# A11 B11 of the transform's first two blocks in seven quarter products, with the gate and T1 of the last stage moved

## The chip, the cores and the metric

The kernel runs on one core of a Trainium2 chip. The metric is the device time of one execution in microseconds. The kernel before took 672.08 us as the median of 3 runs (671.87 to 673.23).

## What is computed

```python
a = einsum("bsd,ed->bse", x, dft_hid_re);  b = einsum("bsd,ed->bse", x, dft_hid_im)
y = einsum("ts,bse->bte", dft_seq_re, a) - einsum("ts,bse->bte", dft_seq_im, b)
up = einsum("bsd,df->bsf", x, w3);  gate = einsum("bsd,df->bsf", x, w1)
z = einsum("bsf,fd->bsd", silu(gate) * up, w2)
g = sigmoid((x * gate_w).sum(-1, keepdims=True))
out = g * y + (1 - g) * z
```

There are 2048 rows (S), 512 columns (D) and 1376 hidden columns of the SwiGLU half. Everything is float32, and w1, w3 and w2 are scaled up by 200.

## The kernel before, in words

Every product is computed in float32 accuracy from two parts of each operand, a high part (ScalarE, `high`, L110) and the rest (VectorE, `low`, L113). `mm3` (L126) then issues three matmuls for each product of tiles: high by high, high by low, low by high, in this order, with the streamed operand's low part first needed by the second of the three. One matmul is 128x128 by 128x512. Each large product is a 2x2 block product done with seven block products instead of eight: P1 to P7, of sums of blocks that are called T1, T2, T3 and T4.

**Stages.** The gate and up projection runs first, in 22 items (`gate_up`, L333), the last of which ends where the transform begins. Four blocks of 512 rows follow for the transform along S (`KIND` "F", blocks 0 to 3), then two blocks for the down projection ("H", 4 and 5), then two for the transform along D ("Y", 6 and 7). A block of the F stage has 28 steps: seven products of four steps each. A step is twelve matmuls on one streamed tile of 128x1024: four in the two halves of the tile by the two output banks, times three.

**The list of steps.** `STEPS` (L650) is written by a loop over blocks, and PE takes the steps in that order, which is also the program's order on every other engine (the schedule is manual). After step m the function `advance` (L755) loads the tile of step m+8 (SP), forms the sum of step m+4 (`sum_c`, VectorE, L723 and L727) and splits step m+3 (`split_c`, high on ScalarE and low on VectorE, into one of four `zo` tiles). So a `zo` tile of step m+3 is the one that step m-1 used. Work of other kinds is hung on steps with `at(blk, n, f)`: it is issued ahead of that step.

**Quarter products.** For blocks 2 and 3 the first product, P1 = A11 B11, isn't done block by block. A11 is the same for both, so the two products are one 2x2 product of quarters of A11 with the two B11, done in seven products m1 to m7 (`QUARTERS`, L645; each has two steps, a and b, of six matmuls) instead of the eight that two P1 hold. The table `AMONG` (L647) sets them between full steps of blocks 1 and 2. `step_quarter` (L913) issues them: m1 and m6, m7 and m4 accumulate in bank 5, and ScalarE copies that bank after m1 (to bank 4, on which m2 accumulates), after m6 and after m7 (to a tile `uu`). m5 goes to bank 7; VectorE then writes bank 6 = bank 7 - uu[0] and bank 7 = bank 7 - uu[1], and m3 accumulates on bank 6. `seeds` (L907) copies the two banks of a block for the later products. Two weights of these products are sums of columns of x (`load_s`, `sums_s`, `high_s`, `low_s`: two tiles `sr`, four subtractions or additions of 128x512 on VectorE, two splits). The streamed sums of quarters are made in DRAM by GpSimd's queue (`quarter_sum`, L440, with accumulating DMAs).

**The last item and the first steps.** In the last `gate_up` item VectorE adds u4 and bank X (L369), which PE must wait for before its last six matmuls on bank X (`prod(x, n, 6, 2, ...)`, L385), since these add to the same bank. Functions hung under `early` (L357) run ahead of that add.

**Results.** A block's four results are multiplied by the gate g on VectorE (`spill`, L947) and stored to DRAM (`zsp`); `load_gate` loads the gate. In the Y stage T1 = B12 + B11 is added on VectorE from two stored blocks.

## Time and profile before

| what | value |
|---|---|
| median of 3 runs | 672.08 us |
| the profiled execution | 671.68 us, of which its span is 669.8 us |
| PE busy | 665.3 us, 99%, 3089 matmuls |
| VectorE busy | 589.6 us, 88%, 699 instructions |
| ScalarE busy | 378.8 us, 57%, 483 instructions |
| DMA | 178.57 MB, 267 GB/s in the mean |
| mean granted TensorE clock | 1.000 |

All times of the trace count from the start of the span. In the timeline a row has its start, how long it lasted, the engine, the line of the kernel, the operation, what it wrote and read, and how often it follows itself; in brackets stands idle time before it and what ended that. Consecutive instructions of VectorE and ScalarE overlap by up to about 0.1 us in the records, so what one costs in a full queue is the distance between two starts. PE's records overlap likewise: six matmuls are shown as 1.46 us and start 1.29 us apart from the next six.

### The profile page before, as it was taken

What the parts mean: (1) busy time and instruction counts of PE and PEld (TensorE: products, weight loads), DVE (VectorE), ACT (ScalarE), POOL (GpSimd) and SP (SyncE); (2) the same over time, 40 slices, a digit from 0 to 9 for tenths busy, and PEclk for the clock granted to TensorE, in tenths of its full rate; (3) what the DMA queues carried; (4) which work ended last, traced back from release to release, by engine and by line L of the source; (5) the groups of instructions that cost most, each with busy time, mean ns of one, the idle gap of its engine ahead of it and who ended that gap; (6) DMA issues with size and microseconds to landing.
All of it is one profiled execution on the core that took longest, in us unless ns stands there. A gap on an engine that the chain in (4) does not pass through costs nothing.

```text
span 669.8 us, 8635 instructions
## 1 busy us (share of the span) xinstructions
PE 665.3 (99%) x3089; PEld 578.4 (86%) x3089; DVE 589.6 (88%) x699; ACT 378.8 (57%) x483; POOL 69.1 (10%) x122
## 2 busy tenths in 40 slices
PE   9999999999999999999999999999999999999997
PEld 6888888888888888888888888888888888888886
DVE  6979987787669999988999998999889799798896
ACT  6765556666546874475565664454447447445452
POOL 0112322221111000112000010001000010010000
PEclk9999999999999999999999999999999999999999
DMA  7789897999996956659668467619989857884942
GB/s 297 263 319 252 298 310 257 281 343 384 425 370 238 389 192 230 215 206 271 254 232 318 157 225 282 231 67 324 405 310 336 270 184 178 314 302 175 339 126 94
DMA packets 49338, 178.57 MB, mean 267 GB/s; under 512 B 5776, under 2 KB 7184, under 8 KB 45840
## 3 DMA queue, kind: packets, MB, share of 16 engines
q1 hardware_dynamic: 35296, 121.52, 51.0%
q0 software_dynamic: 13568, 55.85, 23.9%
q10 hardware_dynamic: 432, 0.66, 0.3%
q8 instruction: 24, 0.39, 0.2%
q14 instruction: 18, 0.15, 0.1%
HBM read 126.35 MB, written 60.04 MB: 278 GB/s over the span
## 4 chain that ended last, share of the span: by engine, by line
PE 99%; ACT 0%; issue 0%
PE P L124 56%; PE X L124 16%; PE quarter L124 12%; PE Z L124 8%; PE Y L124 4%; PE C L124 2%; PE wps L405 1%; PE V L124 0%; PE P4left L124 0%; ACT zc L974 0%
## 5 line engine op out<-in xcount | busy, mean ns | idle before, releaser
L110 ACT ACTIVATE zo<-B 128x1024 fp32r<-128x1024 f32 x178 | 181.0, 1021 | 171.8 <-DVE B L723 67.0
L113 DVE TENSOR_TENSOR zo<-B,zo 128x1024 fp32r<-128x1024 f32 x178 | 208.3, 1178 | 18.5 <-ACT zo L110 17.2
L124 PE MATMUL P<-zo,a 128*128 128x512 f32 x960 | 209.7, 379 | 0.0
L124 PEld LDWEIGHTS P<-zo,a 128*128 128x128 f32 x960 | 181.4, 189 | 25.9
L723 DVE TENSOR_TENSOR B<-B,B 128x1024 f32<-128x1024 f32 (+1 forms) x78 | 91.8, 1177 | 0.1
L124 PE MATMUL P<-zo,H 128*128 128x512 f32 x420 | 91.3, 379 | 0.0
L124 PEld LDWEIGHTS P<-zo,H 128*128 128x128 f32 x420 | 79.2, 189 | 11.8 <-issue 0.7
L124 PE MATMUL X<-xo,wb 128*128 128x512 f32 x378 | 88.7, 379 | 0.0
L124 PEld LDWEIGHTS X<-xo,wb 128*128 128x128 f32 x378 | 71.3, 189 | 10.4 <-DVE u L369 0.2
L124 PE MATMUL quarter<-zo,a 128*128 128x512 f32 x324 | 71.9, 379 | 0.0
L124 PE MATMUL P<-zo,Y 128*128 128x512 f32 (+1 forms) x336 | 71.6, 375 | 0.0
L124 PEld LDWEIGHTS P<-zo,Y 128*128 128x128 f32 x336 | 62.7, 189 | 8.7
L124 PEld LDWEIGHTS quarter<-zo,a 128*128 128x128 f32 x324 | 61.2, 189 | 8.7
L324 POOL DMA_DIRECT2D hsp<-h x40 | 22.3, 558 | 106.5 <-DVE h L375 61.5
L386 ACT ACTIVATE h<-X 128x512 f32<-128x512 f32 x21 | 12.5, 596 | 34.9 <-PE X L124 34.9
L124 PE MATMUL Z<-xo,wb 128*128 128x512 f32 x126 | 30.6, 379 | 0.0
L124 PE MATMUL Z<-xo,wa 128*128 128x512 f32 x126 | 30.6, 379 | 0.0
L727 DVE TENSOR_TENSOR B<-B,B 128x1024 f32<-128x1024 f32 (+1 forms) x26 | 30.6, 1178 | 0.0
L124 PE MATMUL X<-xo,wa 128*128 128x512 f32 x126 | 30.5, 379 | 0.0
L124 PE MATMUL Y<-xo,wa 128*128 128x512 f32 x126 | 30.5, 379 | 0.0
L124 PEld LDWEIGHTS Y<-xo,wa 128*128 128x128 f32 x126 | 23.8, 189 | 3.4
L124 PEld LDWEIGHTS Z<-xo,wb 128*128 128x128 f32 x126 | 23.8, 189 | 3.4
(181 smaller groups left out, 662.1 us busy)
## 6 DMA issues: line engine op xcount, KB each, us to landing
B<-cc SPq DMA_DIRECT2D x64, 512.0 KB, 5.6
hsp<-h POOLq DMA_DIRECT2D x40, 256.0 KB, 6.7
wbsp<-wb POOLq DMA_DIRECT2D x8, 1024.0 KB, 5.8
wb<-wbsp SPq DMA_DIRECT2D x8, 1024.0 KB, 8.2
B<-hsp SPq DMA_DIRECT2D x16, 512.0 KB, 8.1
B<-zsp SPq DMA_DIRECT2D x16, 512.0 KB, 8.7
tsp<-cc POOLq DMA_DIRECT2D x12, 512.0 KB, 9.0
ws<-w SPq DMA_DIRECT2D x11, 512.0 KB, 6.4
```

The costliest lines, as they stand in the source:

```text
L110: nc.scalar.activation(hi, src, AF.Copy)
L113: nc.vector.tensor_sub(lo, src, hi.bitcast(F32))
L124: nc.tensor.matmul(ps.rearrange("p (n a) -> p n a", a=2), u, turns(v)[:, some], **kw)
L324: nc.gpsimd.dma_start(hsp[g, b + k, j // 2, :, j % 2 * 512 : (j % 2 + 1) * 512], h)
L386: nc.scalar.activation(g1, x, AF.Silu)
L405: nc.tensor.matmul(wps, warm[:, :P], warm, start=True, stop=True)
L723: nc.vector.tensor_add(t, t, RAW[blk, b, q][:, :n])
L727: nc.vector.tensor_sub(t, RAW[blk, "B12", q][:, :n], t)
```

## The change

The first products of blocks 0 and 1 are now done as those of 2 and 3 are: `AMONG` gets three entries for block 0, and the loop leaves P1 out for all F blocks.

- Block 0's own P1 had been the first four steps of the stage. Now m1a, m1b, m2a and m2b come first, then two steps of P5 (T1), then m6a, m6b, m7a, m7b, the third step of P5, then m4a, m4b, m5a, m5b, m3a, m3b, and the fourth.
- Each group follows without a full step in between, unlike those of blocks 2 and 3, which keep their places.
- The sums of x for the weights are loaded at the end of item 19 (`load_s0`), and VectorE makes them (`sums_s`) under `early` of the last item. They are split by `high_s` and `low_s` at steps of block 0.
- `quarter_sum` makes 32 sums instead of 16, with other places on GpSimd's queue: 16 during the gate and up projection, 16 at steps of blocks 0 and 1.
- The gate of blocks 0 and 1 is no longer multiplied in there (`PLAIN`); it is done in block 6. The stored B12 of the Y stage is already T1: an accumulating DMA adds it into `zt1` in DRAM, so VectorE's T1 sums of blocks 6 and 7 are gone.
- One late part of w2 moves from block 1 to the end of block 3, where it goes straight into its tile.
- `load_score` and `gates` have later places.

The core of the diff:

```diff
-    QSUMS = [(i, b, h) for i, c, d in ((1, "b12", "b11"), (3, "b12", "b22"), (2, "T1", "b22"),
-                                       (4, "T2", "b21")) for b in (c, d) for h in range(2)]
+    QSUMS = [(j, i, b, h) for j in range(2)
+             for i, c, d in ((1, "b12", "b11"), (2, "T1", "b22"), (3, "b12", "b22"), (4, "T2", "b21"))
+             for b in (c, d) for h in range(2)]
...
-    for n in (3, 4, 5, 6, 8, 9, 10, 11):
+    for n in (1, 3, 4, 5, 6, 8, 9, 10, 11, 19, 20):
         do(mid, n, quarter_sum)
-    for n in (6, 9):
+    for n in (6, 9, 18):
         do(at_end, n, quarter_sum)
...
-    AMONG = {(1, 22): ("m1a", "m1b"), (1, 23): ("m6a",), ...
+    AMONG = {(0, 3): ("m1a", "m1b", "m2a", "m2b"), (0, 5): ("m6a", "m6b", "m7a", "m7b"),
+             (0, 6): ("m4a", "m4b", "m5a", "m5b", "m3a", "m3b"), (1, 22): ("m1a", "m1b"), ...
...
-            if blk in (2, 3) and k == "P1":
+            if blk < NTB and k == "P1":
...
+    def read_s():
+        for i, t in enumerate(SR):
+            nc.sync.dma_start(t, xn[4 * i : 4 * i + 4, :, 256:512].rearrange("k p n -> p k n"))
+
+    def load_s0():
+        SW[:] = [wide(f"sr{i}") for i in range(2)]
+        SR[:] = [t.rearrange("p (k n) -> p k n", k=4) for t in SW]
+        read_s()
...
+    do(at_end, NI - 3, load_s0)
+    for j in range(2):
+        do(early, NI - 1, sums_s, j)
...
-        if b:
+        if b and (KIND[blk], form) != ("Y", "T1"):
             n = cols(blk, q, b)
...
-        elif k == "m2":
-            seeds(2, MB[4], MB[5])
+        elif k == ("m4", "m2")[pair // 2]:
+            seeds(pair, MB[4], MB[5])
...
+            if blk not in PLAIN:
+                g = GT[blk][k // 2] if KIND[blk] == "H" else GT[blk][0]
+                for r in range(2):
+                    nc.vector.tensor_mul(t[:, r], src[r], g)
+            elif ps is not None:
+                for r in range(2):
+                    nc.scalar.activation(t[:, r], ps[r], AF.Copy)
...
+            if k < 2:
+                kw = {"accum_op": ALU.add} if blk % 2 else {}
+                nc.gpsimd.dma_start(zt1[blk // 2, k], flat(t), **kw)
...
+        if 2 * (blk - NTB - 2) + k // 2 in PLAIN:
+            for r in range(2):
+                nc.vector.tensor_mul(t[:, r], src[r], GT[blk][k // 2])
+            ps = None
...
+    for i in range(2):
+        at(0, 2 * i, high_s, i, *(("s1", "u3"), ("c21", "p5"))[i])
+        at(0, (1, 4)[i], low_s, i)
```

**VectorE at the end of the gate and up projection.** `u_21` is the add of L369 of the last item (L370 in the changed kernel), the three rows on `h` end the item, and `zo` are the low parts of the first steps. Before:

```order
L174 SCALAR_TENSOR_TENSOR xr_1819<-xr_1819 128x256 x2
L369 TENSOR_TENSOR u_21_1823<-u_21_1823,X_1663 128x512
L113 TENSOR_TENSOR zo_1849<-B_0_0_1640,zo_1849 128x1024
L374 TENSOR_TENSOR h_1822<-h_1822,Z_1821 128x512
L375 TENSOR_TENSOR h_1822<-s_21_1761,h_1822 128x512
L391 TENSOR_TENSOR h_1822<-h_1822,u_21_1823 128x512
L113 TENSOR_TENSOR zo_1852<-B_0_1_1711,zo_1852 128x1024
L113 TENSOR_TENSOR a_7_1897<-xr_1819,a_7_1897 128x1024
```

Now:

```order
L175 SCALAR_TENSOR_TENSOR xr_1828<-xr_1828 128x256 x2
L783 TENSOR_TENSOR sr_1774<-sr_1773,sr_1774 128x4x128
L784 TENSOR_TENSOR sr_1773<-sr_1773 128x4x128
L786 TENSOR_TENSOR sr_1773<-sr_1774,sr_1773 128x4x128
L787 TENSOR_TENSOR sr_1774<-sr_1774,sr_1773 128x4x128
L370 TENSOR_TENSOR u_21_1832<-u_21_1832,X_1665 128x512
L113 TENSOR_TENSOR zo_1862<-B_0_0_1642,zo_1862 128x1024
L375 TENSOR_TENSOR h_1831<-h_1831,Z_1830 128x512
L376 TENSOR_TENSOR h_1831<-s_21_1765,h_1831 128x512
L392 TENSOR_TENSOR h_1831<-h_1831,u_21_1832 128x512
L113 TENSOR_TENSOR zo_1865<-B_0_1_1714,zo_1865 128x1024
L113 TENSOR_TENSOR a_7_1910<-xr_1828,a_7_1910 128x1024
```

Four operations on `sr` now stand ahead of the add that the last item's matmuls wait for, and so ahead of everything behind it.

**ScalarE in the first steps.** The rows follow the table load that stands ahead of the first step; `zo_1950` before and `zo_1949` now are the high part of T1's first step, whose source is a sum of VectorE. Before:

```order
L110 ACTIVATE zo_1932<-B_0_3_1817 128x1024
L110 ACTIVATE zo_1950<-B_0_0_1872 128x1024
L110 ACTIVATE zo_1968<-B_0_1_1900 128x1024
L110 ACTIVATE zo_1984<-B_0_2_1902 128x1024
L1093 ACTIVATE P_0_0_1987<-P_0_0_1915 128x512
L1093 ACTIVATE P_0_1_1988<-P_0_1_1916 128x512
```

Now (`quarter_1952<-quarter_1928` is the copy of bank 5 to bank 4 between m1 and m2):

```order
L110 ACTIVATE s0s_1925<-sr_1773 128x1024
L110 ACTIVATE zo_1938<-B_0_3_1826 128x1024
L110 ACTIVATE zo_1949<-B_0_0_1885 128x1024
L960 ACTIVATE quarter_1952<-quarter_1928 128x512
L110 ACTIVATE s1c_1954<-sr_1774 128x1024
L110 ACTIVATE zo_1967<-B_0_1_1913 128x1024
```

The copy that m2 needs stands behind the high part of T1's first step.

**PE from m5 to m3.** Before, in blocks 1 and 2: the second step of m5 (bank 7, `quarter_3204`), a full step of block 1, the first of m3 (bank 6, `quarter_3246`):

```order
L124 MATMUL quarter_3204<-zo_3201,s1h 128x512 x2
L124 MATMUL quarter_3204<-zo_3201,s1l 128x512
L124 MATMUL quarter_3204<-zo_3201,s1h 128x512 x2
L124 MATMUL quarter_3204<-zo_3201,s1l 128x512
L124 MATMUL quarter_2950<-zo_3213,a_0_1219 128x512 x3
L124 MATMUL quarter_2950<-zo_3213,a_1_1378 128x512 x3
L124 MATMUL quarter_2926<-zo_3213,a_0_1219 128x512 x3
L124 MATMUL quarter_2926<-zo_3213,a_1_1378 128x512 x3
L124 MATMUL quarter_3246<-zo_3229,s1h 128x512 x2
```

Now, in block 0 (bank 7 is `quarter_2115`, bank 6 `quarter_2136`):

```order
L124 MATMUL quarter_2115<-zo_2097,s1c_1954 128x512 x2
L124 MATMUL quarter_2115<-zo_2097,s1p_1955 128x512
L124 MATMUL quarter_2115<-zo_2097,s1c_1954 128x512 x2
L124 MATMUL quarter_2115<-zo_2097,s1p_1955 128x512
L124 MATMUL quarter_2136<-zo_2108,s1c_1954 128x512 x2
```

And on VectorE, where the two rows on `quarter` are the subtractions between m5 and m3, and the rows ahead of them the low parts of m3a, m3b and of T1's and the sums for T1's and T2's steps:

```order
L113 TENSOR_TENSOR zo_2108<-m_0_0_2028,zo_2108 128x1024
L732 TENSOR_TENSOR B_0_3_2062<-B_0_3_2062,B_0_3_1826 128x1024
L113 TENSOR_TENSOR zo_2123<-m_0_1_2040,zo_2123 128x1024
L732 TENSOR_TENSOR B_0_0_1885<-B_0_0_1885,B_0_0_2064 128x1024
L113 TENSOR_TENSOR zo_2133<-B_0_3_2062,zo_2133 128x1024
L972 TENSOR_TENSOR quarter_2136<-quarter_2115,uu 128x512
L973 TENSOR_TENSOR quarter_2115<-quarter_2115,uu 128x512
```

No full step stands between m5 and m3 in block 0, and the subtractions come behind the low part of T1's fourth step.

More of the change, by code (lines that the diff above doesn't have):

```diff
@@ L830, in late_load @@
     def late_load(i, src, tag):
-        r, m = (flat(ut.tile([P, 2, 512], F32, tag=k, name=f"{k}p{i}"))
-                for k in (tag, "c21" if tag == "u3" else "u2"))
+        r, m = (flat(ut.tile([P, 2, 512], F32, tag=k, name=f"{k}p{i}")) for k in tag)
         nc.sync.dma_start(r, src)
@@ L943, in step_quarter @@
             nc.vector.tensor_sub(MB[7], MB[7], MB["u"][:, 1])
-        elif k == "m3":
+        elif k == "m3" and pair:
             free(SF[1][0])
@@ L989, in load_gate @@
             GT[blk] = [both[:, i] for i in range(2)]
+        elif KIND[blk] == "Y":
+            tbs = list(PLAIN)
+            GT["Y"] = wide("gateY")
+            GT[blk] = [GT["Y"][:, i * 512 : (i + 1) * 512] for i in range(2)]
         else:
```

167 lines of the change are left out of this document (93 added, 74 removed), and 1 row of the table AMONG.

## The prediction

> **What bounds the kernel now.** I read the page first: the busy times, and the chain that ended last.
>
> ```profile
> PE 665.3 (99%) x3089; PEld 578.4 (86%) x3089; DVE 589.6 (88%) x699; ACT 378.8 (57%) x483; POOL 69.1 (10%) x122
> ...
> PE 99%; ACT 0%; issue 0%
> ```
>
> Then the waits of PE alone, whose only row is the start of the kernel, and the chain in order of time, of which one row gives the price of a matmul.
>
> ```profile
> PE wps L405 <- PEq L1324: 0.8, 1, 0.8
> ```
>
> ```profile
> 206.78 132.10 PE P L124 x612
> ```
>
> So PE issues its matmuls without a gap, and the time is their number: 132.10 / 612 = 0.216 us each, 2.59 for a full step of twelve, 1.295 for a quarter step of six. A change gains what it takes off that number, as long as no wait appears. How near the other engines are to that shows by the stretch in which the new steps start (columns: PE, PEld, DVE, ACT, POOL busy, clock, DMA share, GB/s).
>
> ```profile
> 206.78:217.14 10.36, 10.36 (x49) 8.98 (x49) 10.36 (x10) 7.06 (x8) 1.08 (x2) 1.00 0.88 317
> 217.14:227.50 10.36, 10.36 (x50) 9.07 (x49) 10.36 (x11) 8.78 (x11) 0.00 (x0) 1.00 1.02 403
> ```
>
> VectorE has no idle time at all in the first 20.7 us of the transform. PE doesn't wait because VectorE is just in time, and the two timelines show by how little.
>
> ```profile
> 205.32 1.46 PE L124 MATMUL X<-xo,wb 128*128 128x512 f32 x6
> 206.62 18.74 PE L124 MATMUL P<-zo,a 128*128 128x512 f32 x86
> ```
>
> ```profile
> 203.17 0.88 DVE L174 SCALAR_TENSOR_TENSOR xr<-xr 128x256 f32<-128x256 f32 x2
> 204.30 0.69 DVE L369 TENSOR_TENSOR u<-u,X 128x512 f32<-128x512 f32 x1 [0.24 <-PE X L124]
> 204.90 1.22 DVE L113 TENSOR_TENSOR zo<-B,zo 128x1024 fp32r<-128x1024 f32 x1
> 206.04 0.68 DVE L374 TENSOR_TENSOR h<-h,Z 128x512 f32<-128x512 f32 x1
> 206.75 0.69 DVE L375 TENSOR_TENSOR h<-s,h 128x512 f32<-128x512 f32 x1
> 207.45 0.69 DVE L391 TENSOR_TENSOR h<-h,u 128x512 f32<-128x512 f32 x1
> 208.06 1.22 DVE L113 TENSOR_TENSOR zo<-B,zo 128x1024 fp32r<-128x1024 f32 x1
> 209.19 1.22 DVE L113 TENSOR_TENSOR a<-xr,a 128x1024 fp32r<-128x1024 f32 x1
> 210.33 1.22 DVE L113 TENSOR_TENSOR zo<-B,zo 128x1024 fp32r<-128x1024 f32 x1
> 211.46 1.22 DVE L723 TENSOR_TENSOR B<-B,B 128x1024 f32<-128x1024 f32 x1
> 212.60 1.22 DVE L113 TENSOR_TENSOR zo<-B,zo 128x1024 fp32r<-128x1024 f32 x1
> ...
> 214.87 1.22 DVE L113 TENSOR_TENSOR zo<-B,zo 128x1024 fp32r<-128x1024 f32 x1
> ```
>
> Step 0 starts at 206.62, step 1 2.59 later, at 209.21; its low part, which its second matmul needs (209.43), ends at 208.06 + 1.22 = 209.28. That is 0.15 us of room. A wide operation in this full queue costs 1.135 us (210.33 to 211.46).
>
> **The change part by part.**
>
> *Matmuls.* The two P1 were 2 x 48 = 96 matmuls; seven quarter products are 7 x 2 x 6 = 84. Twelve fewer, 3077 in all: 12 x 0.216 = **-2.6 us**. All the rest is waits.
>
> *The four sums at the join.* They stand ahead of the add of L369. The same four stand in block 1 of the trace:
>
> ```profile
> 319.48 0.68 DVE L882 TENSOR_TENSOR sr<-sr,sr 128x512 f32<-128x512 f32 x1
> 320.20 0.69 DVE L883 TENSOR_TENSOR sr<-sr 128x512 f32<-128x512 f32 x1
> 320.81 1.22 DVE L727 TENSOR_TENSOR B<-B,B 128x1024 f32<-128x1024 f32 x1
> ```
>
> One that the next must wait for costs 0.72, the last 0.61: 3 x 0.72 + 0.61 = 2.77. VectorE is free for them at 203.17 + 0.88 = 204.05, so the add starts at 206.8 instead of 204.30 and ends at 207.5. PE's last six on X stood at 205.32 and can't start before: **+2.2 us**, and m1a starts at 206.62 + 2.2 = 208.8. The idle 0.24 us is all that could cover it.
>
> *m1b.* Behind the add VectorE keeps its order: the low part of step 1 comes 208.06 - 204.30 = 3.76 later, at 210.55, and ends at 211.8. But a quarter step lasts 1.295: m1b's turn is at 210.1, and its second matmul waits until 211.8. **+1.5**, and it ends at 212.9.
>
> *m1 to m2.* m2a needs ScalarE's copy of m1's bank. The trace has such a copy, 0.2 us behind the end of the matmuls (338.72 + 12 x 0.216 = 341.31):
>
> ```profile
> 338.72 2.75 PE L124 MATMUL quarter<-zo,a 128*128 128x512 f32 x12
> ```
>
> ```profile
> 341.51 0.58 ACT L931 ACTIVATE quarter<-quarter 128x512 f32<-128x512 f32 x1 [0.19 <-PE quarter L124]
> ```
>
> ```profile
> L110 ACT ACTIVATE zo<-B 128x1024 fp32r<-128x1024 f32 x178 | 181.0, 1021 | 171.8 <-DVE B L723 67.0
> ```
>
> Here the copy stands in ScalarE's queue behind the high part of T1's first step, which needs VectorE's sum. VectorE: low of m1b at 210.55, a_7 at 211.7, low of m2a at 212.8, that sum at 213.95 to 215.2. Then 1.02 for the high part and 0.58 for the copy: 216.85. m2a's turn was 212.9: **+4.0**. m2 then ends at 216.9 + 2.59 = 219.5. VectorE goes on with the low of m2b, the first split of the weights' sums, T1's second sum, and T1's first low at 218.5 to 219.7, in time. Behind the copy ScalarE holds the high parts of the second weights and of T1's second step, which PE takes at 222.1.
>
> *m6 to m7.* Two steps of T1 and m6 end at 219.5 + 3 x 2.59 = 227.3. The copy of m6's bank stands behind the high part of T1's third step, whose sum is VectorE's seventh from 218.5 (six wide ones ahead, 6 x 1.135): 225.3 to 226.5. High part and copy: 228.2. **+1.0**.
>
> *m5 to m3.* m7, T1's third step, m4 and m5 end at 228.3 + 4 x 2.59 = 238.7. m3 accumulates on a bank that VectorE must first write:
>
> ```profile
> 379.19 0.69 DVE L942 TENSOR_TENSOR quarter<-quarter,uu 128x512 f32<-128x512 f32 x1
> 379.79 0.69 DVE L943 TENSOR_TENSOR quarter<-quarter,uu 128x512 f32<-128x512 f32 x1
> ```
>
> ```profile
> 218.31 1.06 ACT L1093 ACTIVATE P<-P 128x512 f32<-128x512 f32 x2
> ```
>
> Ahead of it on VectorE stand the low of m3b, a sum and T1's last low. The low of m3b waits for ScalarE, which has first to do two copies as in the last row, when m4 has ended (236.1 + 0.2 + 1.06 = 237.4), and then m3b's high part: 238.4. Three wide ones bring the subtraction to 241.85, and it ends at 242.5: **+3.9**. From there PE has m3 and T1's last step (to 247.8), VectorE has T2's first low by about 245.4, and the room comes back.
>
> Sum: 2.2 + 1.5 + 4.0 + 1.0 + 3.9 = 12.6 of new waits against 2.6: **+10.0 us**.
>
> *The rest I cost at nothing,* since no engine but PE sets the time there, and PE waits for none. A pair of the gate's products costs 1.2 us (269.88 to the next row at 271.08):
>
> ```profile
> 269.88 1.29 DVE L955 TENSOR_TENSOR zu<-zu,gate 128x512 f32<-128x512 f32 x2
> 271.08 1.22 DVE L113 TENSOR_TENSOR zo<-B,zo 128x1024 fp32r<-128x1024 f32 x1
> ```
>
> Four pairs leave each of blocks 0 and 1, and four enter block 6 (4.8 us); there two wide adds (2.3) take the place of four narrow ones (2.4), and T1's four wide sums in blocks 6 and 7 go (4.5). VectorE idles 3.2 us in the twenty around block 6:
>
> ```profile
> 610.00:620.00 10.00, 10.00 (x48) 8.77 (x47) 8.38 (x9) 4.84 (x7) 0.00 (x0) 1.00 0.26 77
> 620.00:630.00 10.00, 10.00 (x48) 8.77 (x47) 8.37 (x9) 4.11 (x5) 0.00 (x0) 1.00 1.00 346
> ```
>
> Without that room up to 4.7 us would be late there. The part of w2 brings seven narrow operations, about 3 us, to the end of block 3. Block 4 starts at 494.28, its T1 30 matmuls later at 500.76, and that step's low part ends at 497.28: 3.5 us of room, and without it up to 3 would show.
>
> ```profile
> 494.28 35.83 PE P L124 x166
> ```
>
> ```profile
> 496.06 1.22 DVE L113 TENSOR_TENSOR zo<-B,zo 128x1024 fp32r<-128x1024 f32 x1
> ```
>
> The first pair's last sums in DRAM leave GpSimd in item 20, ahead of two items' stores of h that only block 4 reads; if one came late, SP would hold the load of m4 and all loads behind it.
>
> *A rule against the change.* The first matmuls of the kernel show what PE does from rest: 0.425 us each, twice the usual.
>
> ```profile
> 0.78 4.68 PE L405 MATMUL wps<-const-bfloat16-1.0 128*128 128x512 bf16 x11 [0.78 <-PEq L1324]
> ```
>
> The Trainium skill (TensorE: Matmul & The Clock Gate, Part 1: The HAM clock gate) says that PE's clock falls to half after about one idle window of 3.4 us, free-running, and rises after as much work. Two of my waits, 4.0 and 3.9, are that long; by the rule each could cost some 1.7 us, an estimate from that page. No pause of that length lies inside this trace, which can't tell.
>
> **The rivals.**
>
> *Nothing waits (faster).* VectorE makes the sums in its idle time before 204.30, the copies come at once, and the 2.6 stay: 671.7 - 2.6 = 669.1. It decides at 205.32: the add must be written by then. For it: VectorE idles a little in each item. Against it: its idle time there is 0.24 us, and the sums stand behind, not in, the earlier gaps. 0.08.
>
> *Only the turnarounds.* The queues are short when the copies' turn comes, so that m2, m7 and m3 wait only for 0.2 + 0.58, again 0.8, and 0.3 + 0.69: 2.6 us. With the 2.2 at the join that is 4.8 - 2.6 = +2.2, 674; 0.10. If the join is free too, the gain is used up: 672; 0.04.
>
> *The clock.* As in the sum, but PE restarts slowly behind the two long waits, each time as in the row above: 11 x (0.425 - 0.216) = 2.3: 682.1 + 4.6 = 686.7. The page above states the rule for it. 0.10.
>
> *The loads.* The tiles of T1 and m6 wait for the item stage's memory to come free:
>
> ```profile
> SPq L753 <- PE X L124: 13.4, 1, 13.4
> ```
>
> ```profile
> 206.81 1.28 SPq L753 DMA_DIRECT2D B<-cc  x3
> ```
>
> They now go out 2.2 us later, with ten more tiles in the same 30 us, while DMA was at 1.02 of its time in the second stretch above. At half of 403 GB/s a tile of 0.52 MB takes 2.6, and the sixth ends 16 us after 209, near 225, or 227 with the issue, and T1's third sum (225.3) is 2 late, or 4 if the next wait is also hit: up to 686. For me against it: the waits themselves give DMA 10 us more. 0.10.
>
> **How the numbers follow.** My forecast has 0.58. The profiled execution took 671.68, so 681.7; the median is 0.4 above it: 672.08 + 10.0 = **682.1**. Its own range, about half a us either way on each of the five waits, is 679 to 684.5. The range 674 to 687 leaves out the cases at 669 and 672 (0.12) and some edges. 0.2% (1.3 us) is about what a measurement of this kernel can tell. Faster: 0.08, same: 0.04, slower: 0.88.
>
> **What would show it.** In the changed profile PE's busy time falls by about 2.6 us, and PE's waits, empty until now, name VectorE at the last X, ScalarE's copies at m2 and m7, and VectorE's subtraction at m3, all between 205 and 243. T2's first step of block 0 starts near 248. I am wrong if PE stays gapless there, if DMA ends the waits, or if a gap appears after 250.

## The result and the profile after

The changed kernel takes 705.48 us (median of 4 runs, 703.71 to 706.43) against 672.19 for the kernel before on the same chip: ratio 1.0494, 95% interval 1.0482 to 1.0507. It is slower by 33.3 us, where 10 were forecast. The profiled execution took 706.43 with a span of 704.7 us, 34.9 more than before.

Some words first. The *join* is the place where the last item's six matmuls on bank X meet the first step of block 0. xr_7 is the last tile of x that is loaded to become a weight (an A tile), sr are the two tiles for the sums of x, and a B or m tile is a streamed tile of a full step or of a quarter step. A *zo part* is the high or the low part of a streamed tile. The xr, sr, B and m tiles take their memory from one set of equal buffers (`F4`), so a load can start only when an earlier tile's last reader is done.

The page's busy times, and its row of the granted clock in 40 slices of 17.6 us:

```profile
PE 674.3 (96%) x3077; PEld 581.5 (83%) x3077; DVE 594.3 (84%) x699; ACT 393.2 (56%) x503; POOL 82.3 (12%) x138
...
PEclk9999999999996989999899999999999999999999
```

The twelve matmuls are gone (3077), yet PE is busy 674.3 us instead of 665.3, +9.0 where -2.6 was due, so PE's rows are 11.6 us longer than their number asks for. The clock row, full in every slice before, has dips in slices 13, 15 and 20. The rest of the 34.9 is idle time: 704.7 - 674.3 = 30.4 against 4.5, +25.9. PE's waits, but for those at the kernel's start (waited for: us in total, times, longest):

```profile
PE X L124 <- DVE u L370: 9.7, 1, 9.7
PE quarter L124 <- DVE quarter L972: 5.4, 1, 5.4
PE quarter L124 <- ACT zo L110: 4.1, 1, 4.1
PE quarter L124 <- ACT quarter L960: 3.7, 1, 3.7
PE quarter L124 <- DVE zo L113: 1.1, 2, 0.6
...
PE quarter L124 <- ACT uu L963: 0.7, 1, 0.7
```

PE's timeline tells where they lie and how the matmuls behind them ran (start, us, in brackets the idle time before):

```profile
216.33 2.93 PE L124 MATMUL X<-xo,wb 128*128 128x512 f32 x6 [9.69 <-DVE u L370]
...
221.81 1.35 PE L124 MATMUL quarter<-zo,a 128*128 128x512 f32 x5 [0.64 <-DVE zo L113]
226.87 4.48 PE L124 MATMUL quarter<-zo,a 128*128 128x512 f32 x12 [3.71 <-ACT quarter L960]
...
255.95 1.19 PE L124 MATMUL quarter<-zo,s1c 128*128 128x512 f32 x2 [5.43 <-DVE quarter L972]
...
332.66 0.79 PE L124 MATMUL quarter<-zo,a 128*128 128x512 f32 x1 [4.10 <-ACT zo L110]
333.92 10.52 PE L124 MATMUL quarter<-zo,a 128*128 128x512 f32 x35 [0.47 <-DVE zo L113]
```

Six matmuls on X took 1.46 in the kernel before and take 2.93 behind the wait of 9.7; the twelve of m2 took 4.48 where twelve take 2.75 elsewhere; the last 35 of the list took 10.52, and 48 take that at full clock. So four places have a wait and a slow stretch behind it: the join (205 to 221), m2 (223 to 231), m3 (250 to 261), and a place that the forecast doesn't have, block 1 at 328 to 344. From the rows, the matmuls in these stretches ran 1.9, 1.7, 2.5 and 3.2 us longer than at full clock, 9.3 in all. The other 2.3 of the 11.6 lie elsewhere. Some 1.2 of them, by estimate, are only the way in which the record shows a stop: six matmuls are shown as 1.46 us and start 1.29 apart, 0.17 less, and there are seven stops. The rest has no cause shown here.

The chain that ended last shows what the join waited for (start, us):

```profile
197.54 13.99 DMA xr<-xn
211.55 0.44 DVE xr L173
...
215.59 0.69 DVE u L370
```

So behind the name of VectorE's add in the list of waits stands a load, that of xr_7, for which VectorE stood idle 7.60 us, and then the four sums on sr. At m3 the chain goes back to a load too, that of the B tile of T1's last step:

```profile
238.91 11.64 DMA B<-cc
```

But VectorE's own rows ahead of the subtraction, and ScalarE's row that released them, say how little that load alone was worth:

```profile
246.81 1.06 ACT L110 ACTIVATE zo<-m 128x1024 fp32r<-128x1024 f32 x1 [1.51 <-DMA m<-tsp]
```

```profile
247.90 2.51 DVE L113 TENSOR_TENSOR zo<-m,zo 128x1024 fp32r<-128x1024 f32 x2 [1.35 <-ACT zo L110]
250.57 1.23 DVE L732 TENSOR_TENSOR B<-B,B 128x1024 f32<-128x1024 f32 x1 [0.16 <-DMA B<-cc]
251.71 1.22 DVE L113 TENSOR_TENSOR zo<-m,zo 128x1024 fp32r<-128x1024 f32 x1
...
255.12 0.69 DVE L972 TENSOR_TENSOR quarter<-quarter,uu 128x512 f32<-128x512 f32 x1
```

VectorE waited 0.16 us for the B tile. From 247.90 on it works with no other gap: the low parts of m5b and m3a, the sum on that B tile, the low part of m3b, one more sum, T1's last low part, and then the subtraction. Two loads that came late, m5b's tile and the B tile, set the start of this queue, within 0.16 us of each other; its length does the rest.

In block 1 PE waits for a zo part, and that for ScalarE. ScalarE's and GpSimd's timelines and SP's waits there:

```profile
306.73 1.07 ACT L989 ACTIVATE zs<-P 128x512 f32<-128x512 f32 x2
...
330.60 1.06 ACT L854 ACTIVATE s1g<-s1g 128x1024 f32<-128x1024 f32 x1 [11.26 <-DMA s1g<-gs]
```

```profile
299.01 1.11 POOL L449 DMA_DIRECT2D tsp<-tsp  x2
...
310.60 0.89 POOL L449 DMA_DIRECT2D tsp<-cc  x1 [3.42 <-DMA tsp<-tsp]
311.15 0.91 POOL L993 DMA_DIRECT2D zsp<-zs  x1
311.70 0.90 POOL L996 DMA_DIRECT2D zt<-zs  x1
```

```profile
SPq L837 <- DMA zt<-zs: 16.5, 1, 16.5
```

Read backwards: the Sigmoid of gates(1) stood 11.3 us in ScalarE's queue, with the zo parts behind it; its score was loaded late because the load writes the buffer s1, which zs_0 held until its store had landed; and that store stood in GpSimd's queue behind a sum in DRAM.

### The profile page after: what moved, and what is told of

It is laid out like the page before. It is cut to its first block, busy times and chain, and to the rows that moved or that the text cites. A ratio compares the mean times of both kernels' runs of the same rounds, so it can differ in the third digit from the quotient of the medians.

```text
span 704.7 us, 8688 instructions
## 1 busy us (share of the span) xinstructions
PE 674.3 (96%) x3077; PEld 581.5 (83%) x3077; DVE 594.3 (84%) x699; ACT 393.2 (56%) x503; POOL 82.3 (12%) x138
## 4 chain that ended last, share of the span: by engine, by line
PE 86%; DMA 9%; ACT 2%; DVE 2%; issue 1%; POOL 0%; SPq 0%; DVEq 0%; ACTq 0%; POOLq 0%
PE P L124 40%; PE quarter L124 19%; PE X L124 15%; PE Z L124 7%; PE Y L124 4%; DMA xr<-xn 2%; DMA B<-cc 2%; DMA tsp<-tsp 2%; DMA s1g<-gs 1%; DMA zt<-zs 1%; PE C L124 1%; DMA xs_B<-xt 1%; ACT zo L110 1%; DVE zo L113 1%; PE V L124 0%
## 5 line engine op out<-in xcount | busy, mean ns | idle before, releaser
L110 ACT ACTIVATE zo<-B 128x1024 fp32r<-128x1024 f32 x174 | 177.0, 1021 | 154.6 <-DVE B L732 68.3
L113 DVE TENSOR_TENSOR zo<-B,zo 128x1024 fp32r<-128x1024 f32 x174 | 203.6, 1178 | 31.6 <-ACT zo L110 30.2
L124 PE MATMUL quarter<-zo,a 128*128 128x512 f32 x648 | 149.4, 389 | 8.9 <-ACT zo L110 4.1
L124 PEld LDWEIGHTS quarter<-zo,a 128*128 128x128 f32 x648 | 125.9, 195 | 29.3 <-ACT zo L110 4.5
L124 PE MATMUL P<-zo,a 128*128 128x512 f32 x576 | 127.1, 379 | 0.0
L124 PEld LDWEIGHTS P<-zo,a 128*128 128x128 f32 x576 | 108.9, 189 | 15.5
L124 PEld LDWEIGHTS X<-xo,wb 128*128 128x128 f32 x378 | 72.0, 191 | 20.6 <-DVE u L370 10.3
L732 DVE TENSOR_TENSOR B<-B,B 128x1024 f32<-128x1024 f32 (+1 forms) x74 | 87.0, 1175 | 0.3 <-DMA B<-cc 0.2
L736 DVE TENSOR_TENSOR B<-B,B 128x1024 f32<-128x1024 f32 (+1 forms) x26 | 30.6, 1177 | 0.0
L113 DVE TENSOR_TENSOR zo<-m,zo 128x1024 fp32r<-128x1024 f32 x20 | 24.4, 1222 | 5.4 <-ACT zo L110 5.3
L110 ACT ACTIVATE zo<-m 128x1024 fp32r<-128x1024 f32 x20 | 21.1, 1056 | 11.3 <-PE P L124 4.5
```

The costliest lines, as they stand in the source:

```text
L110: nc.scalar.activation(hi, src, AF.Copy)
L113: nc.vector.tensor_sub(lo, src, hi.bitcast(F32))
L124: nc.tensor.matmul(ps.rearrange("p (n a) -> p n a", a=2), u, turns(v)[:, some], **kw)
L732: nc.vector.tensor_add(t, t, RAW[blk, b, q][:, :n])
L736: nc.vector.tensor_sub(t, RAW[blk, "B12", q][:, :n], t)
```

## The experiments

Theory at this point: four causes that add up, namely loads at the join, PE's empty queue between a quarter product and the copy of its bank, the score's chain in block 1, and the clock. Rivals: the moved gate and T1 cost the time by themselves; the DMA engines are full, so that a wait that is removed comes back elsewhere.

**The moves alone.** Blocks 0 and 1 get their own A11 B11 steps back, without the sr work and the 16 sums in DRAM that went with the quarter products; the gate, T1 of the last stage and w2's late part stay moved.

```diff
-    AMONG = {(0, 3): ("m1a", "m1b", "m2a", "m2b"), (0, 5): ("m6a", "m6b", "m7a", "m7b"),
-             (0, 6): ("m4a", "m4b", "m5a", "m5b", "m3a", "m3b"), (1, 22): ("m1a", "m1b"),
+    AMONG = {(1, 22): ("m1a", "m1b"),
...
-            if blk < NTB and k == "P1":
+            if blk in (2, 3) and k == "P1":
-    do(at_end, NI - 3, load_s0)
```

> The moves alone: the gate of blocks 0 and 1 and T1 of the last stage stay as in the changed kernel, blocks 0 and 1 get their own A11 B11 steps back, with no sr loads and sums ahead of block 0 and no GpSimd sums for these blocks. Theory one (the quarter products, the loads that they put ahead of T1 and the sums that they put into GpSimd's queue cost all but a few us): the join waits as before, under 1.5 us, block 0 has no wait above 1 us, the score's load for gates(1) starts about 3 us earlier, so that TensorE's stop near 330 is at most 2 us of the 5; time 672 to 677. Rival (the moved gate with its score load is at fault by itself): the stop near 330 stays at 4 to 5 us with its half clock, time 679 to 682. Second rival (the moves cost most of the 33 us): 695 or more.

Measured: 671.7 us, ratio 0.9992 (0.9983 to 1.0002). PE waits only at the kernel's start, 0.8 and 0.3 us:

```profile
PE 665.0 (99%) x3089; PEld 579.5 (87%) x3089; DVE 581.0 (87%) x685; ACT 384.4 (57%) x492; POOL 70.5 (11%) x122
```

Better than theory one asked: the moves cost nothing, and all 33 us come with the quarter products and their loads and sums. The score's chain is in this kernel too, in the same order, and does no harm:

```profile
270.35 1.07 ACT L985 ACTIVATE zs<-P 128x512 f32<-128x512 f32 x2
...
293.23 1.04 ACT L850 ACTIVATE s1g<-s1g 128x1024 f32<-128x1024 f32 x1
```

From zs_0's end (271.4) to the Sigmoid's turn (293.2) pass 21.8 us; in the changed kernel they are 307.8 and 330.60 - 11.26 = 319.3, 11.5 us. The 10.3 us between are the four steps of 2.59 that block 1 lost: with its A11 B11 steps gone, what is hung on its step 6 comes that much sooner after block 0's results.

**gates(1) later.** Four steps, the time that block 1 lost.

```diff
-    for g, n in enumerate((18, 6)):
+    for g, n in enumerate((18, 10)):
-    at(1, 12, load_s)
+    at(1, 14, load_s)
```

> gates(1) four steps later (steps 10 to 13 of block 1 in place of 6 to 9), and the sr tiles that reuse its buffer s1 with it (load 14 for 12, sums 17 and 18 for 15 and 16, high part 19 for 18, low part 21 for 20). Theory one (TensorE's stop of about 5 us at 328 to 334 is the Sigmoid of gates(1) standing in ScalarE's queue for the score's load, which waits for the store of zs_0 behind GpSimd's sums): Sigmoid comes some 10 us later and finds its load done, the stop and its half clock (3.4 us of matmul time) go, time 705.5 - 8 = 696 to 699. Rival (the later sr load is now late itself, or the stop is the zo parts' own load): a stop of 3 us or more at another place of block 1, and the time within 3 us of 705.5.

Measured: 696.03 us, ratio 1.0355 (1.0340 to 1.0371), 9.5 less than the changed kernel. Theory one holds. Part of the gain, 1.6 us, lies elsewhere: the waits on X and at m3 were 9.1 and 4.4 in the profiled execution, for 9.7 and 5.4. The same 48 matmuls follow without a gap, and the Sigmoid hardly waits:

```profile
323.39 10.52 PE L124 MATMUL quarter<-zo,a 128*128 128x512 f32 x48
```

```profile
328.01 1.06 ACT L854 ACTIVATE s1g<-s1g 128x1024 f32<-128x1024 f32 x1 [0.72 <-DMA s1g<-gs]
```

**GpSimd's sums of block 0 sooner,** the other end of the same chain.

```diff
-    for n in (13, 15, 17, 19, 21, 23, 25):
+    for n in (11, 12, 13, 14, 15, 16, 17):
         at(0, n, quarter_sum)
```

> Only GpSimd's queue is changed: block 0's seven DRAM sums at steps 11 to 17 instead of 13 to 25, so that none stands between the gate's stores and the stores of zs_0. In the changed kernel zs_0 was ready at 307.8 us and its store left at 311.2, behind a sum that waited for another sum's landing. Theory one (GpSimd's queue is part of the chain to the score's load): the score's load starts some 3.4 us sooner, ScalarE's wait for it falls from 11.3 to about 8 and TensorE's stop near 330 from about 5 to about 2 us; time 705.5 - 3 to - 5 = 700.5 to 702.5. Rival (the store lands when the full DMA engines let it): the stop stays within 1 us of 5 and the time within 1 us of 705.5.

Measured: 702.11, ratio 1.0443 (1.0427 to 1.0459), 3.4 less. The stop in block 1 is down to 1.1 us, as theory one has it and more. But the wait ahead of m3 grew from 5.4 to 8.9:

```profile
PE quarter L124 <- DVE quarter L972: 8.9, 1, 8.9
...
PE quarter L124 <- ACT zo L110: 1.1, 1, 1.1
```

What was moved up runs among T1's loads: no store holds GpSimd's queue at that place, so three of the sums leave at 239.8 to 247.1, and T1's last B tile landed 17.4 us after its issue instead of 11.6. Here VectorE stood idle 2.32 us for it.

**xr_7's load first,** ahead of the sr loads.

```diff
-    do(at_end, NI - 2, load_a, NG - 1)
+    do(at_end, NI - 3, load_a, NG - 1)
```

> The last A part's load xr_7 is put ahead of the two sr loads, so that it takes the F4 buffer that is free first; nothing else moves. Theory one (the join's 9.7 us is xr_7's load, issued 14 us later than before because the sr tiles took the earlier buffers): TensorE's wait for u falls from 9.7 to 2 to 3 us (the four sr sums and their own load stay), the half clock behind it (1.9 us of matmul time) goes, since the wait is short; time 705.5 - 7 to - 9 = 696 to 699. Rival (the DMA engines are full between 185 and 210, so that whichever load goes last is late and the sr sums wait in its place): the wait stays over 7 us and the time within 2 us of 705.5.

Measured: 702.4, ratio 1.0443 (1.0425 to 1.0460), 3.1 less. The wait on X is 6.8, and the rival is nearly right: the second of the sr loads, issued at 190.3, landed 18.7 us later and holds VectorE now.

```profile
209.12 0.69 DVE L783 TENSOR_TENSOR sr<-sr,sr 128x512 f32<-128x512 f32 x1 [4.69 <-DMA sr<-xn]
```

**xr_7 first and the sr sums behind the join.**

```diff
-    for j in range(2):
-        do(early, NI - 1, sums_s, j)
...
+        at(0, 1, sums_s, i)
```

> As the run with xr_7's load first, and the four sr sums taken from ahead of the last item's add to the second quarter step of block 0 (high and low parts of s0 and s1 two and one steps later too). Theory one (with both loads out of VectorE's queue ahead of that add nothing is left that the join waits for): the wait of 9.7 us on X falls to under 1.5 and its half clock (1.9 us) goes; time 705.5 - 9 to - 11 = 694.5 to 696.5. Rival (the sr tiles hold their F4 buffers longer, and their load lands no sooner; the wait comes back at m6, whose s0 parts are late, or at a later T1 step): the waits between 205 and 262 still sum to over 15 us of the 20, time 700 or more.

Measured: 696.21, ratio 1.0349 (1.0329 to 1.0369), 9.3 less: the wait on X is gone, theory one holds in its size. What stays of block 0:

```profile
PE quarter L124 <- ACT quarter L958: 5.6, 1, 5.6
PE quarter L124 <- DVE quarter L970: 4.7, 1, 4.7
```

The wait ahead of m2 grew by 1.9, which is the rival's part in it.

**The sr work alone.** The kernel with the moves alone, plus the sr loads and sums, used by nothing.

> The other way round: the run with the moves alone (671.7, blocks 0 and 1 with their own A11 B11 steps, no quarter products of theirs) with the sr work of the changed kernel put back: the two sr loads ahead of xr_7's, the four sums ahead of the last item's add, and their buffers given back at the second and fifth step of block 0. Nothing uses the sums. Theory one (the sr loads and sums alone make the join wait, whatever follows): TensorE waits 8 to 11 us on X as in the changed kernel, with the half clock behind it (1.9 us), and little else, since block 0's first steps cover later tiles; time 671.7 + 10 to + 13 = 682 to 685. Rival (the join waits because the quarter products' own tiles m compete): the wait is 4 us or less, time under 677.

Measured: 675.06, ratio 1.0044 (1.0030 to 1.0059), 3.4 more than with the moves alone. Theory one falls here: the wait on X is 2.0, not 9.7. The rival's numbers came; its reason, the product tiles m, is left to the next run, which has them.

```profile
208.72 1.56 PE L124 MATMUL X<-xo,wb 128*128 128x512 f32 x6 [2.00 <-DVE u L370]
```

xr_7's load left at 197.5 us in the changed kernel and at 197.6 here, since the sr tiles take its F4 buffer in both (in the kernel before it left at 183.4). It landed after 13.99 us there and after some 6 here. What differs is the traffic it left into: the stretch from 200 to 210, of the changed kernel and then of this one (PE, PEld, DVE, ACT, POOL, clock, DMA share, GB/s):

```profile
200.00:210.00 10.00, 6.63 (x31) 5.48 (x29) 3.21 (x4) 3.68 (x5) 1.43 (x3) 0.98 1.05 347
```

```profile
200.00:210.00 10.00, 8.00 (x38) 6.70 (x37) 9.00 (x14) 3.68 (x5) 1.08 (x2) 1.00 0.53 191
```

GpSimd's last sums for blocks 0 and 1 leave at 190.8 to 199.4 us in the changed kernel, and this one has none.

**Those three sums early,** at items 11 to 13.

```diff
-    for n in (1, 3, 4, 5, 6, 8, 9, 10, 11, 19, 20):
+    for n in (1, 3, 4, 5, 6, 8, 9, 10, 11, 12, 13):
-    for n in (6, 9, 18):
+    for n in (6, 9, 11):
```

> Only GpSimd's queue is changed, the other way: the last three DRAM sums for blocks 0 and 1 (items 18 to 20, on the trace at 190.8 to 199.4 us) go to items 11 to 13, before 150 us. The sr loads and xr_7's order stay. Theory one (the join is late by traffic: without any of these sums xr_7's load, issued at the same 197.6 us, let TensorE wait 2.0 us and not 9.7): the wait on X falls to 3 to 5 us, its half clock (1.9 us) goes in part or whole; time 705.5 - 5 to - 9 = 696.5 to 700.5. Rival (the F4 buffer that xr_7 waits for decides, and the engines stay full because the sums only push other loads later): wait over 7 us, time within 3 us of 705.5.

Measured: 703.96, ratio 1.0461 (1.0442 to 1.0479), only 1.5 less. The wait on X is 2.0 as in the run before, with the product tiles m in the kernel, so the traffic of these sums is what made it 9.7, and the rival of the run before falls. But the half clock behind it stayed:

```profile
214.57 2.10 PE L124 MATMUL X<-xo,wb 128*128 128x512 f32 x6 [2.00 <-DVE u L370]
216.47 4.10 PE L124 MATMUL quarter<-zo,a 128*128 128x512 f32 x12
```

Six take 1.46 and twelve 2.75 at full clock. And the sums now push another load late, and with it the item at 144:

```profile
144.61 5.49 PE L124 MATMUL X<-xo,wb 128*128 128x512 f32 x12 [3.57 <-DVE u L370]
```

```profile
142.62 0.42 DVE L155 TENSOR_TENSOR w2m<-w2r 128x256 f32<-128x256 f32 x1 [5.33 <-DMA w2r<-w]
```

The wait costs 3.6 and its half clock (5.49 instead of 2.75) 2.7. The rival has the time right, theory one the wait on X.

**Fillers in PE's waits.** 77 matmuls that compute nothing stand where PE waited.

```diff
+        if n == last:
+            dummy(bank(3, "warm"), 40, start=True, stop=True)
         prod(x, n, 6, 2, False, True)
...
+        if pair == h == 0 and k == "m2":
+            dummy(bank(3, "warm"), 15, start=True, stop=True)
```

> The kernel with 77 more bf16 matmuls of 128x512 that compute nothing of the output: 40 ahead of the last six matmuls on X, 15 ahead of m2a, 22 (zeros added to a bank) ahead of m3a, so that TensorE does not stand still in the three long waits at the start of block 0. Nothing else is changed; at 0.216 us they fill 8.6, 3.2 and 4.8 us of waits of 9.7, 3.7 and 5.4. Theory (the clock halves because TensorE stood still, and the half clock cost the matmuls behind these waits 1.9 + 1.7 + 2.5 = 6.1 us): the six on X take 1.46 us again instead of 2.93, the twelve of m2 2.75 instead of 4.48; the waits' ends stay, time 705.5 - 6 = 698 to 701. Rival (the clock falls for another reason, such as the load on the chip): the half clock stays and the time is within 1 us of 705.5. Second rival (the fillers push the real matmuls back): slower by up to 3 us.

Measured: 701.9, ratio 1.0437 (1.0422 to 1.0453), 3.6 less with 77 matmuls more.

```profile
PE 684.5 (98%) x3154; PEld 585.0 (84%) x3154; DVE 593.9 (85%) x699; ACT 392.9 (56%) x503; POOL 82.3 (12%) x139
```

```profile
214.97 1.56 PE L124 MATMUL X<-xo,wb 128*128 128x512 f32 x6 [0.62 <-DVE u L375]
...
224.23 2.86 PE L124 MATMUL quarter<-zo,a 128*128 128x512 f32 x12 [0.42 <-ACT quarter L972]
```

Without the fillers' 77 x 0.216 = 16.6 us PE is busy 667.9, 6.4 less than in the changed kernel, where 6.1 was expected: the six on X take 1.56, m2's twelve 2.86. So the half clock behind these three waits is shown to come from PE's standing still. Of the 6.4 only 3.6 reach the time: the zo parts, for which PE waited 1.1 us, are now waited for 3.6.

**The quarter steps interleaved with T1.**

```diff
-    AMONG = {(0, 3): ("m1a", "m1b", "m2a", "m2b"), (0, 5): ("m6a", "m6b", "m7a", "m7b"),
-             (0, 6): ("m4a", "m4b", "m5a", "m5b", "m3a", "m3b"),
+    AMONG = {(0, 3): ("m1a", "m1b"), (0, 4): ("m2a", "m2b", "m6a", "m6b"),
+             (0, 5): ("m7a", "m7b", "m5a", "m5b"), (0, 6): ("m4a", "m4b", "m3a", "m3b"),
```

> The quarter steps of blocks 0 and 1 in another order among the four steps of T1: m1, T1, m2 m6, T1, m7 m5, T1, m4 m3, T1, so that other matmuls stand between a product and the copy or subtraction of its bank; the two small loads' splits keep their places. Theory one (m2a waits 3.7 us and m3a 5.4 us for the copy and the subtraction of a bank, because TensorE has nothing else in its queue): m2a's wait falls to about 3.7 - 2.6 = 1.1 us, m3a's and m7a's to under 1, and the half clocks behind them (1.7 and 2.5 us) go; time 705.5 - 8 to - 11 = 694 to 698. Rival (loads: the parts of T1's third and fourth step and of the products come when their F4 buffers and the DMA engines let them, and end the wait in the copy's place): a wait of 4 us or more between T1's second and last step put down to a zo part or a B tile, time 701 or more.

This kernel leaves out one thing, the sum of T1's first tile, a VectorE add of 1.2 us. Measured: 701.29, ratio 1.0439 (1.0421 to 1.0457), 4.2 less. The waits for the copy and the subtraction are gone, as theory one has it. Half of the gain isn't there, and the time is the rival's, since T1's tiles are late, and one holds PE in the subtraction's place:

```profile
246.00 0.80 PE L124 MATMUL quarter<-zo,s1c 128*128 128x512 f32 x1 [3.54 <-DVE zo L113]
```

```profile
243.58 1.23 DVE L732 TENSOR_TENSOR B<-B,B 128x1024 f32<-128x1024 f32 x1 [5.44 <-DMA B<-cc]
```

**All four edits:** xr_7 first, the sr sums behind the join, interleaved, gates(1) later.

> All together: xr_7's load first, the sr sums behind the join, the interleaved order, and gates(1) four steps later. Theory one (the 35 us of span are these four waits, the half clock behind them, less 2.6 for the twelve matmuls): no wait of TensorE above 1.5 us, the clock full throughout; 672.1 - 2.6 + 1 to 4 of small waits = 670.5 to 674. Rival (the 14.7 MB more of loads, stores and sums move through DMA engines that are already full between 185 and 310, so that loads end other waits when these go): waits of 8 us or more remain in blocks 0 and 1 and the time is 678 or more.

This kernel leaves out the same sum. Measured: 682.89, ratio 1.0164 (1.0149 to 1.0179), 22.6 less than the changed kernel. The single gains add up: 9.3 + 4.2 + 9.5 = 23.0. But it isn't 670 to 674, and the rival's waits of over 8 us are there (9.0 us for zo parts, the longest 4.6).

**The same with that sum put back** and the sr tiles' buffers freed a step sooner.

> As the run with all four edits, but with the sum of T1's first tile, which the two runs with the interleaved order left out, put back (one VectorE add, 1.2 us), and with the sr sums and the parts of s0 and s1 one quarter step sooner, so that the two F4 buffers of the sr tiles come free about 2.6 us sooner. In the run before, TensorE's longest wait (4.6 us at 235) was a B tile that left when the part s0u had freed an sr buffer and landed 14.1 us later, and its half clock followed. Theory one (buffer and load in line): that wait falls to about 2 us and its half clock goes; time 682.9 - 3 to - 6 = 677 to 680. Rival (the load lands with the full DMA engines, not by its issue): within 1.5 us of 682.9.

Measured: 682.61, ratio 1.0155 (1.0140 to 1.0171). The 4.6 fell to 1.6, as theory one has it, but the time stayed, which is the rival's number and not its reason. Two things changed at once: at the first steps, where the run before had waits of 1.0 and 0.7, there is now one of 2.0 as well, and a half clock behind it. It is for the high part of T1's first tile, for which ScalarE waited 3.2 us, until VectorE had made the sum that was put back.

```profile
209.86 1.35 PE L124 MATMUL quarter<-zo,a 128*128 128x512 f32 x5 [1.04 <-DVE zo L113]
213.22 0.48 PE L124 MATMUL P<-zo,a 128*128 128x512 f32 x1 [2.01 <-ACT zo L110]
214.48 4.33 PE L124 MATMUL P<-zo,a 128*128 128x512 f32 x11 [0.77 <-DVE zo L113]
```

**The same without the sr loads and sums,** the operands made from tiles that lie there.

```diff
-    do(at_end, NI - 3, load_s0)
...
+            SR.append(A1[i][:, 0].bitcast(F32))
```

> As the mended run with all edits, but without the operands' own work for block 0: the two sr tiles are neither loaded nor summed, and the parts s0 and s1 are made from two A tiles that lie there already (the high and low parts are still made, and every matmul stands). It leaves that part of the computation out. Theory one (what is left above the kernel before, some 10 us, is the sr tiles: two F4 buffers held in the stretch in which loads land 14 to 19 us late, and 2.8 us of VectorE): T1's tiles leave as early as in the kernel before, waits of block 0 under 3 us in all, time 670 to 674, at or below the kernel before. Rival (the eight product tiles m and their DRAM sums, the other 1 MB each way, keep the DMA engines behind): waits of over 5 us at zo parts whose tile is m or B stay, time 676 or more.

Measured: 679.51, ratio 1.0112 (1.0097 to 1.0127). The sr work is worth 3.1 us of the 10.4 that were left. The other 7.3 stay, so theory one falls for them. The rival's signs came (679.51, and 6.0 us of waits for zo parts), its reason is not shown for the first steps: VectorE works without a gap from 204.85 to 212.10, and no load ends the wait of 2.0 there. The waits of PE from 200 to 260 us are for parts:

```profile
PE quarter L124 <- DVE zo L113: 2.8, 3, 1.1
PE P L124 <- ACT zo L110: 2.0, 1, 2.0
PE P L124 <- DVE zo L113: 1.2, 2, 0.7
```

**The sums moved out of T1's loads.** With gates(1) later and the three sums early, block 0's seven sums go into block 1.

```diff
-    for n in (13, 15, 17, 19, 21, 23, 25):
-        at(0, n, quarter_sum)
-    for n in (4, 6, 8, 9, 11, 12, 14, 16, 18):
+    for n in (0, 1, 2, 3, 4, 5, 6, 7, 8, 9, 10, 11, 12, 14, 16, 18):
         at(1, n, quarter_sum)
```

> The run with gates(1) later (696.0), with the last three sums for blocks 0 and 1 early as in the run beside it, and the seven sums of block 0's steps, of which four ran at 221 to 233 us among T1's loads since nothing in GpSimd's queue held them, put into block 1 behind the gate's stores. Theory one (DRAM sums among the loads of the join and of T1 cost there): the wait on X falls from 9.1 to 3 to 5 us, the one ahead of m3a from 4.4 to about 2, and half clocks with them; time 696.0 - 7 to - 12 = 684 to 689. Rival (the waits are set by F4 buffers coming free, not by traffic): time 692 or more. Second rival (the seven sums now delay the stores and loads of block 1): a wait over 3 us behind 300 us.

Measured: 708.26, ratio 1.0535 (1.0514 to 1.0556). The second rival holds. The join's wait is 2.0 and m3's 3.8, but block 1 now has one of 13.8: the store of the gate waits behind the sums in GpSimd's queue, the second pair of sr tiles wants the buffer of that store, and VectorE stands 19 us for their load. SP's list of waits has 29.5 us for the landing of the gate's store; in the row of VectorE the profile names another DMA, which landed at the same moment.

```profile
362.80 10.43 PE L124 MATMUL P<-zo,a 128*128 128x512 f32 x35 [13.78 <-DVE zo L113]
```

```profile
360.19 0.69 DVE L783 TENSOR_TENSOR src<-srs,src 128x512 f32<-128x512 f32 x1 [19.35 <-DMA tsp<-cc]
```

**All edits and the sums moved.**

> The mended run with all four edits (682.6), and the sums moved in both ways. Theory one (what is left is in part the sums' traffic among T1's loads): the waits of block 0 fall from 10 us in all to 5 to 7, the short half clock goes, time 676 to 680. Rival (VectorE and ScalarE are the rest: the parts of the product tiles m, s0 and s1 come one after another at 1.2 us each, faster than TensorE's 2.6 us per step only on the average): the waits put down to zo parts stay over 8 us, time 681 or more. By neither is it below the kernel before, 672.

Measured: 702.76, ratio 1.0456 (1.0441 to 1.0472). Neither case came: the same stop, 15.5 us here, hides what the edits gain in block 0. No version with the quarter products of blocks 0 and 1 was faster than the kernel before; the best of them that leaves nothing out took 682.61.

## Why the prediction went wrong

Its direction was right, and so was the kind of wait at the places that it named. It failed in three steps: block 1, which it costed at nothing, the clock, which it left out of its sum, and the join, which it mis-sized. Two of its own signs of being wrong came, a load behind the wait on X and a gap after 250. Term by term, in us:

| term | forecast | trace |
|---|---|---|
| join, wait on X | 2.2 | 9.7 |
| m1b | 1.5 | 0.6 |
| m1 to m2 | 4.0 | 3.7 |
| m6 to m7 | 1.0 | 0.7 |
| m5 to m3 | 3.9 | 5.4 |
| block 1, 328 to 334 | 0 | 4.6 |
| PE's busy time | -2.6 | +9.0 |

**What held.** The waits of PE for ScalarE's copies came within 0.3 us of the queue counting, and PE's matmuls were the bound of the kernel before: the moves of the gate and of T1, costed at nothing, cost nothing (0.9992). Some of the nearness is luck. On the way to m2 VectorE stood idle 1.19 us for ScalarE's h, which the count doesn't have, and PE came to m2 later too, because its matmuls ran 1.9 us slow. The same slowness hid part of m1b's wait, 0.6 for 1.5.

**"The four sums at the join ... +2.2 us."** The term is right for what it counts: the sr work alone made the join wait 2.0, and in the changed kernel the four sums and the add stand in the trace as counted (212.81 to 215.59, 2.78 us). It failed because it takes xr_7 as there at 204. The sr tiles took xr_7's buffer, so that its load left 14 us later than before, which the runs show to be harmless by itself. "The first pair's last sums in DRAM leave GpSimd in item 20" was weighed only for m4 and the loads behind it, not as traffic; with the DMA share at 1.05 they pushed xr_7's landing out to 211.5. Without these sums the wait was 2.0, in all three runs that kept the sr work ahead of the join and took the sums away. That term is 7.5 us short.

**"The rest I cost at nothing, since no engine but PE sets the time there."** This is the step that failed in block 1, where the waits were 4.6 us and the slow stretch behind them cost 3.2. Each moved piece was asked where it stands now, but not how far apart two pieces stand once four steps between them are gone. The score's load needs a buffer that block 0's result holds; 21.8 us of room became 11.5. Giving back the four steps gave 9.5 us.

**m5 to m3.** The size is near (5.4 for 3.9), and most of the reason holds. The subtraction stands 3.4 us behind the start of m3b's low part (251.71 to 255.12), three wide operations, as counted. But that low part started 1.2 us behind m5's end, where the count had it 0.3 ahead of it, and this is the 1.5 that was missing: the queue ahead of it began late, by the loads of m5b's tile and of T1's last B tile. To that extent the rival of the loads was right on this place. It got 0.10 because the waits were thought to give the loads time. They do, but the buffers come free in the same chain: the B tile's load left at 238.9, when a low part of VectorE had ended, and took 11.6 us.

**The clock.** The rival had it at 0.10 and 4.6 us for two waits. It is shown by the fillers for three places and by the run with gates(1) later for the fourth, and it is larger: 9.3 us in four places. The Trainium skill (TensorE: Matmul & The Clock Gate, Part 1: The HAM clock gate) says that the gate watches a free-running window of 3.4 us and halves the clock after an idle one. The trace agrees: its record of the clock has half speed in four stretches of 10.24, 3.41, 6.83 and 6.83 us, whole multiples of 3.41, each starting in a wait and outlasting it; their starts lie 17.07, 27.31 and 78.51 us apart, whole multiples too, as they would with a free-running window. That a whole window must be idle, the runs don't bear out (see the last section). I had given the rule a price (1.7 each) and left it out of the sum, although the sum itself contained two waits longer than the window.

So 12.1 us of waits were missing (24.7 for 12.6) and 11.6 of PE's busy time, of which 9.3 are the clock: 23.7 of the 24.9 by which the span outgrew the forecast. What stays open are the 7.3 us of the kernel without the sr loads: they go with waits for zo parts in VectorE's and ScalarE's queues and a half clock behind the first of them, but no run takes that work away, so that this is argued from the rows and not shown.

## What to carry to other kernels

When a change removes steps, list the pairs of events that these steps kept apart, above all a buffer's last reader and its next writer, and take the removed time off each pair's room. A stretch in which the DMA engines are full has no free load: price a new transfer by which waiting load it pushes back, and look for it in every queue that nothing holds back, GpSimd's too. On a PE that never paused, a wait of 2 us or more should be charged for itself and, as a risk, for the matmuls that may run at half clock behind it, here 1.7 to 3.2 us each time; whether they do depends on where the wait falls, as the next section shows.

## What the runs showed of the hardware

A half clock doesn't need one long wait, and a long wait doesn't always bring one. In the kernel with all edits and T1's sum put back, waits of 1.04, 2.01 and 0.77 us with a few matmuls between them were followed by eleven matmuls in 4.33 us instead of some 2.5. In the run with those three sums early, the join's wait of 2.0 us was followed by half clock; in the run with the sr work alone, the same wait was not. In the run with GpSimd's sums of block 0 sooner, m2 waited 3.71 us, and its twelve matmuls took 2.86 us, at full clock.

The records of the clock put these in order. In every run the clock changes only at points that lie whole multiples of 3.41 us apart. If each trace is cut at these points, PE's rows give the idle time in each window. In all the traces of this case taken together, the clock fell to half behind each of the 33 windows in which PE was idle for 59% or more, some 2.0 us of 3.41, and behind none in which it was idle for 57% or less. The wait of 3.71 us just named was cut by a window's edge into 57% and 52%, the harmless one of 2.0 us into 51% and less, while the other 2.0 us lay within one window. This limit is worked out from these traces alone, and the ends of PE's rows are modelled, so it is an estimate.

The Trainium skill (TensorE: Matmul & The Clock Gate, A second HAM failure mode: psum-queue depth-cycling) tells of short pauses between groups of matmuls that make the clock swing. This case agrees with that in the three short waits above.

With the waits filled by matmuls that compute nothing, the record shows full clock through all of block 0. And loads of 0.5 MB that left while the DMA share was 1.0 landed 11.6 to 23.1 us later (xr_7 and the B tile in the changed kernel, the B tile with the sums sooner, the two sr loads with xr_7 first), where xr_7 took some 6 us at a share of 0.84, so that the issue time told little about the arrival.
